# A second plain column block, the sums of activations after the attention, float32 gate tiles, and a scheduler that knows a shared SBUF interface

## The chip, the cores and the metric

The kernel runs on one core of a Trainium2 chip. The metric is the time on the device in microseconds (us), lower is better. TensorE is called PE here, VectorE DVE, ScalarE ACT, GpSimd POOL and SyncE SP, as in the profile.

## The reference

Causal attention, then two MLPs on the 896 tokens (2 batches of 448), all results in float32:

```python
# q, k, v: (2, 12, 448, 64)
scores = scale * np.matmul(q, k.transpose(0, 1, 3, 2))
scores = np.where(mask, -1000000000.0, scores)      # mask: upper triangle
attn = np.exp(scores - max); attn = attn / (sum + 1e-09)
x = np.matmul(attn, v)                              # to (896, 768)
g = x @ w_gate                                      # (768, 1536)
x = (g * (1.0 / (1.0 + np.exp(-g))) * (x @ w_val)) @ w_out    # (1536, 768)
h = x @ w_in                                        # (768, 2048)
out = (h * np.clip(h + 3.0, 0.0, 6.0) / 6.0) @ w_out2         # (2048, 768)
```

The weights come in float64 and are read as pairs of 32-bit words.

## The kernel before

**Number format.** A float32 operand of a matmul is split into a high part (fp32r) and a low part, the difference: ACT casts the high part, DVE or POOL subtracts it. A product of two split operands is three matmuls. A weight tile is loaded raw by SP (768 KB, two tiles `raw` that take turns), ACT scales its high words into `w`, DVE shifts `w` and joins the low words to it, and then it is split into `whi` and `wlo`.

**Attention.** 12 pairs of heads (6 of each batch), in steps woven by hand: scores `sc`, exponentials `e`, transposes `tp` and `et`, products `pv`, normalised rows `xn`, their transposes `tr` into 448 columns, split into the tiles `x` (`xt_parts`). For the MLP's Strassen form `xt_parts` also makes sums and differences of the `x` tiles: POOL adds the two parts of a tile into `xa` or `xb` (L627), DVE forms the differences (L631, L634 to L636), and the tiles `t1` are split there (`split_x`). The tile framework orders the instructions of this part by its own priorities.

**First layer (w_gate, w_val).** The 12 column blocks of 128 are planned in `mlps` by `Plan`: each operation is entered with the engines that may do it, its cost there, and what it reads and writes; PE's order is fixed as entered, due times are counted back from PE's, and a list scheduler places every other operation on the engine where it can start first, earliest due first. From 9 us of the plan's own time on, the engines' queues keep that order. Column block 0 (`PLAIN = 1`) is plain: gate and value, each of two batches, 18 matmuls of 448 columns each, 72 in all. Its two weight tiles are loaded and prepared in the attention (`UNIT_AT`). Blocks 1 to 11 are in Strassen-Winograd form: the 2 by 2 split is batches by halves of the 768 inputs and gate by value; 7 products of 9 matmuls, 63 in all, in the order a11 (x tiles), s3 with `t3`, s2 with `t2`, s1 with `t1`, a12, a22 with `t4`, s4. Their weight operands come from `operands`: 4 sums and 7 splits of 384 columns on DVE or POOL for each block. The results are combined on DVE (`tmp`, `mm`) and gated (`silu` on ACT, then a product). For the first four blocks (`EARLY = 4`) the gate's result is split at once from PSUM; for the others it is kept as a float32 tile `g` and split at the end of the layer (`g_parts`) into `gh` and `gl`.

**The rest.** The layer of w_out is planned too (6 column blocks, in two parts of 384 and 512 tokens); the second MLP is written in order, with the next weight tiles made ahead.

Instructions of the planned part have the line of the helper `InOrder`, L53, whatever they do; they are told apart by their tiles. The scheduler's main rule is this one, for each engine e:

```python
t = max(free_at[e], min(at[i] for i in mine))
i = min((i for i in mine if at[i] <= t), key=lambda i: (due[i], i))
```

Of the kernel before, what the change touches and what calls it, by code (L numbers as in the profile page):

```python
# [69 lines left out]
class Plan:  # L70
# [4 lines left out]
    def op(self, where, call, reads=(), writes=()):  # L75
# [19 lines left out]
        self.ops.append((where, call, before, ready))  # L95

    def run(self, emit):
# [3 lines left out]
        for i, (_, _, before, _) in enumerate(ops):  # L101
            for j in before:
                after[j].append(i)
# [3 lines left out]
        for i, (where, _, _, _) in enumerate(ops):  # L107
# [11 lines left out]
        free_at = dict(START)  # L119
# [4 lines left out]
        while waiting:  # L124
            best = None
            for e in free_at:
# [7 lines left out]
                t = max(free_at[e], min(at[i] for i in mine))  # L134
                i = min((i for i in mine if at[i] <= t), key=lambda i: (due[i], i))
# [5 lines left out]
            free_at[e] = t + cost  # L141
            if e in ("pe", "sp"):
                (pe_order if e == "pe" else sp_order).pop(0)
            placed.append((t, len(placed), i, e))
            for j in after[i]:
                left[j] -= 1
                at[j] = max(at[j], t + cost + LAG[e])
# [9 lines left out]
def tile_attention_glu_mlp(  # L157
# [123 lines left out]
    for f in range(PLAIN):  # L281
        units.append((cols(w_gate, f), KD, 128))
        units.append((cols(w_val, f), KD, 128))
# [41 lines left out]
    xs = {}  # L325
# [23 lines left out]

    def split_x(k, h, by):  # L350

        (xa, _), (xb, _) = sums[h], more_sums[h]
        src = {1: xb[:, 1], 2: xa[:, 0], 3: xa[:, 1], 4: xb[:, 0]}[k]
        xs[k, h] = pair_tile(f"t{k}{h}")
        t = xs[k, h][0]
        act.copy(t[:, 0], src)
        by.tensor_tensor(out=t[:, 1], in0=src, in1=t[:, 0].bitcast(F32), op=ALU.subtract)

    def attention():
        with ExitStack() as st:  # L360
# [241 lines left out]
            def xt_parts(p):  # L602
# [7 lines left out]
                def one(c):  # L610
# [12 lines left out]
                    h = hp % HD  # L623
                    (xa, _), (xb, _) = sums[h], more_sums[h]
# [50 lines left out]
    def mlps():  # L675
# [41 lines left out]
        def floats(src, name):  # L717
# [27 lines left out]
            plan.op({"vec": 0.75}, shift, writes=[w])  # L745
            plan.op({"vec": 1.15}, join, reads=[raw], writes=[w])
            return w

        def parts_of(src, hi, lo, size, both=True):
# [6 lines left out]
            where = {"vec": 0.08 + size * 0.0012}  # L756
            if both:
                where["pool"] = 0.1 + size * 0.0027
# [5 lines left out]
                reads=[(s, s_part), (h, h_part)], writes=[(l, l_part)],  # L764
            )

        def combine(where, out, in0, in1, op):
# [4 lines left out]
                reads=[a[:2], b[:2]], writes=[o[:2]],  # L772
# [8 lines left out]
        x1s = [[here(x1[b][k], 6.5 if (b, k) == (1, KD - 1) else 0.0) for k in range(KD)] for b in range(B)]  # L781
        t1 = [here(xs[1, h], 2.0) for h in range(HD)]
        xa = [here(sums[h], 7.8 if h == HD - 1 else 0.0) for h in range(HD)]
        xb = [here(more_sums[h], 7.8 if h == HD - 1 else 0.0) for h in range(HD)]
# [6 lines left out]
        def gate(f, b, bank_, in0, in1):  # L791
# [9 lines left out]
            parts_of(at(bank_, None, tok), at(hi, b, mid), at(lo, b, mid), S, both=False)  # L801
# [37 lines left out]
        def operands(f):  # L839
# [5 lines left out]
            either = {"vec": 0.65, "pool": 1.2}  # L845
# [7 lines left out]
            combine(either, s1, a21, a22, ALU.add)  # L853
            piece("a11", a11)
            combine(either, a21, a11, a21, ALU.subtract)
            piece("s3", a21)
            combine(either, s2, s1, a11, ALU.subtract)
# [3 lines left out]
            combine(either, a12, a12, s2, ALU.subtract)  # L861
# [4 lines left out]
        g_tiles(0)  # L866
        ws = [[Spot(real=t) for t in made[u]] for u in range(2)]
        used[0] += 2
        for b in range(B):
            got = []  # L870
            for wh, wl in ws:
                t, n = bank_spot()
                got.append((t, n))
                plan.op(
                    {"pe": 3 * KD * PE448},
                    lambda e, t=t, wh=wh, wl=wl, b=b: mm3(
                        tok(t()),
# [190 lines left out]
```

## Time and profile before

| | |
|---|---|
| time, median of 3 runs | 609.87 us (609.69 to 610.8) |
| the profiled execution's own time | 610.62 us |
| its span | 608.5 us |
| mean granted clock of PE | 0.994 |
| busy share: PE, DVE, ACT, POOL | 98%, 63%, 48%, 41% |
| chain that ended last, largest shares | PE 80%, DVE 12%, POOL 3%, issue 2% |
| read from HBM | 61.73 MB |

The profile is of one execution. The span runs from its first to its last instruction; the execution's own time includes what lies around that. A window is given in us from the span's start. "Idle before" is the time that the engine sat without work before an instruction, and the name behind the arrow is what ended it. An x9 in a timeline merges nine instructions of one kind.

### The profile page before, as it was taken

How to read it: one execution, taken by the hardware profiler on the slowest of the kernel's cores; microseconds unless marked ns; L12 is line 12 of the kernel's file. 1: busy time of each engine (PE TensorE's matmuls, PEld its weight loads, DVE VectorE, ACT ScalarE, POOL GpSimd, SP SyncE). 2: the span in 40 equal slices, each digit the busy share in tenths (PEclk: the TensorE clock that was granted, in tenths of full speed). 3: DMA queues.
4: the chain of work that ended last, by engine and by line, in shares of the span. 5: the costliest groups of instructions: out<-in, count | busy, mean ns of one | idle time of the engine just before them, and what ended most of it. 6: DMA issues, size and time to landing. Idle time of an engine off the chain costs nothing.

```text
span 608.5 us, 9429 instructions
## 1 busy us (share of the span) xinstructions
PE 595.2 (98%) x3519; PEld 551.1 (91%) x3519; DVE 382.1 (63%) x741; ACT 293.6 (48%) x530; POOL 246.8 (41%) x194
## 2 busy tenths in 40 slices
PE   8999999997999999999999999999999999999997
PEld 5999998886999998989888889999888899999997
DVE  6889899889999999989754443544555531123001
ACT  5677786665655645547432224555555532223000
POOL 4566766267658877748100002222222222223200
PEclk9999999997999999999999999999999999999999
DMA  9555546044334435341543343333333343342002
GB/s 180 131 127 141 135 104 173 13 155 140 108 106 155 157 111 181 124 156 53 160 156 111 120 121 106 108 106 103 104 103 104 104 110 111 118 156 66 1 0 92
DMA packets 83918, 70.15 MB, mean 115 GB/s; under 512 B 35232, under 2 KB 79776, under 8 KB 83872
## 3 DMA queue, kind: packets, MB, share of 16 engines
q1 hardware_dynamic: 83872, 69.55, 39.5%
q8 instruction: 28, 0.46, 0.3%
q14 instruction: 18, 0.15, 0.1%
HBM read 61.73 MB, written 2.75 MB: 106 GB/s over the span
## 4 chain that ended last, share of the span: by engine, by line
PE 80%; DVE 12%; POOL 3%; issue 2%; ACT 1%; DMA 0%; SPq 0%; DVEq 0%; ACTq 0%; POOLq 0%
PE mm L53 65%; PE pv L580 5%; PE sc L509 4%; PE tp L552 3%; DVE w L53 2%; DVE v L53 2%; POOL s L53 1%; DVE s L53 1%; PE tr L434 1%; DVE tmp L53 1%; POOL a L53 1%; DVE e L522 1%; DVE qq L447 1%; PE tr L614 1%; DVE mm L53 1%
## 5 line engine op out<-in xcount | busy, mean ns | idle before, releaser
L53 POOL TENSOR_TENSOR wlo<-w,whi 128x768 fp32r<-128x768 f32 (+1 forms) x33 | 59.4, 1801 | 243.9 <-PE mm L53 219.6
L53 DVE TENSOR_SCALAR w<-w 128x768 uint32<-128x768 uint32 (+1 forms) x58 | 39.7, 685 | 79.3 <-ACT w L53 78.7
L53 ACT CAST whi<-w 128x768 fp32r<-128x768 f32 (+1 forms) x47 | 38.5, 818 | 78.8 <-PE mm L53 72.7
L53 PE MATMUL mm<-whi,g2l 128*128 128x384 f32 x224 | 74.8, 334 | 0.0
L53 PE MATMUL mm<-whi,g2h 128*128 128x384 f32 x224 | 74.8, 334 | 0.0
L53 PE MATMUL mm<-wlo,g2h 128*128 128x384 f32 x224 | 74.8, 334 | 0.0
L580 PE MATMUL pv<-v,et 112*112 112x65 f32 x480 | 73.5, 243 | 0.8 <-DVE et L558 0.8
L53 PE MATMUL mm<-x2h,wlo 128*128 128x384 f32 (+1 forms) x192 | 69.9, 364 | 0.0
L53 PE MATMUL mm<-x2l,whi 128*128 128x384 f32 (+1 forms) x192 | 69.8, 364 | 0.0
L53 PE MATMUL mm<-x2h,whi 128*128 128x384 f32 (+1 forms) x192 | 69.6, 362 | 0.0
L53 PE MATMUL mm<-t,s 128*128 128x448 f32 x297 | 65.6, 378 | 3.5 <-ACT s L53 2.1
L580 PEld LDWEIGHTS pv<-v,et 112*112 112x112 f32 x480 | 65.5, 177 | 2.2 <-DVE et L558 1.0
L53 PEld LDWEIGHTS mm<-t,s 128*128 128x128 f32 x297 | 57.5, 194 | 9.9 <-ACT s L53 2.5
L53 ACT ACTIVATE w<-raw 128x768 f32<-128x768 f32 (+1 forms) x58 | 51.5, 890 | 29.5 <-POOL wlo L53 19.2
L552 PE MATMUL tp<-ident,e 112*112 112x112 f32 x240 | 61.1, 260 | 2.3 <-ACT e L532 2.2
L53 DVE SCALAR_TENSOR_TENSOR w<-raw,w 128x768 uint32<-128x768 uint32 (+1 forms) x58 | 59.7, 1029 | 0.9
L532 ACT ACTIVATE e<-e,m 112x336 f32<-112x336 f32 (+1 forms) x96 | 48.7, 531 | 20.8 <-DVE m L522 20.6
L53 PE MATMUL mm<-gh,wlo 128*128 128x384 f32 (+1 forms) x144 | 52.5, 364 | 0.0
L53 PE MATMUL mm<-gl,whi 128*128 128x384 f32 (+1 forms) x144 | 52.4, 364 | 0.0
L53 PE MATMUL mm<-gh,whi 128*128 128x384 f32 (+1 forms) x144 | 52.2, 362 | 0.0
L53 PE MATMUL mm<-x,a 128*128 128x448 f32 x198 | 44.2, 367 | 0.0
L522 DVE CUSTOM_DVE_ANT_0 e<-sc,mask 112x336 f32<-112x336 f32 (+1 forms) x96 | 40.7, 445 | 4.5 <-PE sc L509 2.6
(126 smaller groups left out, 1322.6 us busy)
## 6 DMA issues: line engine op xcount, KB each, us to landing
raw<-in_moe_w_out_dram SPq DMA_DIRECT2D x28, 768.0 KB, 4.3
raw<-in_moe_w_in_dram SPq DMA_DIRECT2D x16, 768.0 KB, 4.5
raw<-in_moe_w_gate_dram SPq DMA_DIRECT2D x12, 768.0 KB, 4.2
raw<-in_moe_w_val_dram SPq DMA_DIRECT2D x12, 768.0 KB, 5.6
kn<-in_k_dram SPq DMA_DIRECT2D x24, 112.0 KB, 2.6
qn<-in_q_dram SPq DMA_DIRECT2D x24, 112.0 KB, 2.6
v<-in_v_dram SPq DMA_DIRECT2D x12, 224.0 KB, 3.2
out_dram<-ob SPq DMA_DIRECT2D x14, 192.0 KB, 1.8
```

Of the source, the lines that this page charges most:

```text
L53: ins = call(*args, **kw)
L434: nc.tensor.transpose(tr[:, c * C : (c + 1) * C], n[:, c].rearrange("p j d -> p (j d)"), ident[:C, :C])
L447: nc.vector.tensor_copy(hi[r, j, :], f[r, :])
L509: nc.tensor.matmul(sp[:C, o : o + w], t["qq"][:, j, c * C : (c + 1) * C], t[("kk", "k2")[i]][:, j, 0:w], start=(i == 0), stop=(i == 1),)
L522: nc.vector.tensor_tensor_reduce(out=es, in0=sp[:C, o : o + w], in1=mask[:, S - w :], op0=ALU.add, op1=ALU.min, scale=-SCALE, scalar=3.0e3 ...
L532: nc.scalar.activation(out=es, in_=es, func=AF.Exp, scale=-1.0, bias=m[:, x : x + 1])
L552: nc.tensor.transpose(tp[:C, at - lo : at - lo + C], e[:, at : at + C], ident[:C, :C])
L580: nc.tensor.matmul(box["o"][:, qc, :], et[:, at : at + C], vt[:, j, c, :], start=(c == 0), stop=(c == qc))
L614: nc.tensor.transpose(tr[:, c * C : (c + 1) * C], xn[:, c].rearrange("p j d -> p (j d)"), ident[:C, :C])
```

## The change

Five things change.

1. `PLAIN = 2`: column block 1 is plain too. Its weight tiles are loaded and split in the plan (`unit`), not in the attention.
2. The sums of activations leave the attention. `xt_parts` now copies each transposed tile on ACT into `xa` or `xb` (12 copies) and makes one difference on DVE for half of the pairs of the second batch. The other nine differences and the splits of `t1` are operations of the plan, on DVE or POOL.
3. `EARLY = 0`: every gate tile is kept in float32 and split by `g_parts`.
4. The planner has a flag `port` on the operations that read and write SBUF alone: of these only one runs at a time, on DVE or on POOL. Its costs of DVE and POOL operations, the start times and the due times between PE operations are other numbers.
5. `unit` and the plain block become functions used for both cases.

```diff
-PLAIN = 1
+PLAIN = 2
-START = {"act": 5.6, "vec": 7.9, "pool": 7.0, "pe": 0.0, "sp": 0.0}
+START = {"act": 6.5, "vec": 7.2, "pool": 7.3, "pe": 0.0, "sp": 0.0}
-EARLY = 4
+EARLY = 0
...
+                t = min(t + LAG["pe"], due[j]) if "pe" in ops[i][0] and "pe" in ops[j][0] else t
...
-                t = max(free_at[e], min(at[i] for i in mine))
-                i = min((i for i in mine if at[i] <= t), key=lambda i: (due[i], i))
+                starts = {i: max(free_at[e], at[i], port_free if ops[i][4] else 0.0) for i in mine}
+                t = min(starts.values())
+                i = min((i for i in mine if starts[i] <= t), key=lambda i: (due[i], i))
...
+            if ops[i][4]:
+                port_free = t + cost
...
-                    whole = xa[:, b] if hp < HD else xb[:, 0] if b == 0 else None
-                    if whole is not None:
-                        nc.gpsimd.tensor_tensor(
-                            out=whole, in0=x[:, 0].bitcast(F32), in1=x[:, 1].bitcast(F32), op=ALU.add
-                        )
+                    xa, xb = sums[hp % HD][0], more_sums[hp % HD][0]
+                    nc.scalar.copy((xa if hp < HD else xb)[:, b], src)
                     if b == 1 and hp < HD:
-                        nc.vector.tensor_tensor(out=xb[:, 1], in0=src, in1=xa[:, 0], op=ALU.subtract)
-                        split_x(1, h, pool)
-                    if b == 1 and hp >= HD:
-                        nc.vector.tensor_tensor(out=xa[:, 0], in0=src, in1=xb[:, 1], op=ALU.subtract)
-                        nc.vector.tensor_tensor(out=xa[:, 1], in0=src, in1=xa[:, 1], op=ALU.subtract)
-                        nc.vector.tensor_tensor(out=xb[:, 0], in0=xb[:, 0], in1=xa[:, 0], op=ALU.subtract)
+                        nc.vector.tensor_tensor(out=xa[:, 0], in0=src, in1=xa[:, 0], op=ALU.subtract)
...
+        plain(0, [[Spot(real=t) for t in made[u]] for u in range(2)])
         used[0] += 2
+        for f in range(1, PLAIN):
+            plain(f, [unit(cols(w, f), both=True) for w in (w_gate, w_val)])
+        tk = {}
+        for h in range(HD):
+            f1, f2, f3, f4 = at(xa[h], 0, nth(0)), at(xb[h], 1, nth(1)), at(xa[h], 1, nth(1)), at(xb[h], 0, nth(0))
+            by = {"vec": 0.58, "pool": 1.25}
+            combine(by, f3, f2, f3, ALU.subtract, port=True)
+            combine(by, f2, f2, f1, ALU.subtract, port=True)
+            combine(by, f4, f4, f2, ALU.subtract, port=True)
+            for k, src in ((1, f1), (3, f3), (2, f2), (4, f4)):
                 t = take([128, 2, S], F32R, f"t{k}{h}")
                 parts_of(src, at(t, 0, nth(0)), at(t, 1, nth(1)), S)
-                tk[k].append(t)
+                tk.setdefault(k, []).append(t)
...
-        for f in range(1, K1):
+        for f in range(PLAIN, K1):
```

How the built program's queues move, at three places.

*First: DVE at the end of the attention* (`x` is the split of a transposed tile, `et` the copy of a transposed exponential that the next `pv` reads, `w` the first weight tile in halves). Before:

```order
L53 TENSOR_TENSOR x_1877<-tr_1837,x_1877 128x448
L634 TENSOR_TENSOR xa_68<-tr_1837,xb_71 128x448
L635 TENSOR_TENSOR xa_68<-tr_1837,xa_68 128x448
L636 TENSOR_TENSOR xb_71<-xb_71,xa_68 128x448
L53 TENSOR_SCALAR w<-w 128x384
L558 COPY et<-tp_1906 112x336
L53 SCALAR_TENSOR_TENSOR w<-raw,w 128x384
L590 TENSOR_SCALAR r<-pv_1904 112x4
```

With the change:

```order
L53 TENSOR_TENSOR x_1868<-tr_1828,x_1868 128x448
L552 COPY et<-tp_1895 112x336
L53 TENSOR_SCALAR w<-w 128x384
L584 TENSOR_SCALAR r<-pv_1893 112x4
L53 SCALAR_TENSOR_TENSOR w<-raw,w 128x384
L586 RECIPROCAL ri<-r 112x4
L53 TENSOR_TENSOR xa_68<-xb_71,xa_68 128x448
L587 TENSOR_TENSOR xn<-pv_1893,ri 112x4x64
```

The three differences of `xa` and `xb` are gone from between the split of `x` and the copy `et`; one difference stands five places behind `et`.

*Second: ACT at the start of the plain block* (`whi` is the cast of a weight tile, in two halves of 384 and then one of 768; `tmp<-mm` is the silu of the first plain product). Before:

```order
L53 CAST x_1953<-tr_1939 128x448
L53 ACTIVATE w<-raw 128x768
L53 CAST whi<-w 128x384
L53 ACTIVATE w<-raw 128x384
L53 CAST whi<-w 128x384
L53 CAST whi<-w 128x768
L53 CAST x_1974<-tr_1969 128x448
L53 ACTIVATE w<-raw 128x768
L53 CAST t_2036<-xa_68 128x448
```

With the change:

```order
L53 CAST whi<-w 128x384
L53 ACTIVATE w<-raw 128x384
L53 CAST t_2047<-xa_68 128x448
L53 CAST x_1942<-tr_1928 128x448
L53 CAST whi<-w 128x384
L618 COPY xb_72<-tr_1928 128x448
L53 ACTIVATE w<-raw 128x768
L53 CAST x_1961<-tr_1956 128x448
L53 CAST t_2050<-xa_69 128x448
L53 ACT_TABLE_LOAD
L53 ACTIVATE tmp_2044<-mm_1977 128x448
L53 CAST whi<-w 128x768
```

The load of ACT's function table and the first silu now stand ahead of the cast of the second weight tile; before, they stood 17 places behind it.

*Third: PE in the attention, a stretch that returns in six pairs of heads* (`sc` scores, `tr` transposes of k and q, `tp` of exponentials). Before:

```order
L434 MATMUL tr_565<-ident,kn 128x112
L509 MATMUL sc_576<-kk_103,qq_102 112x224
L509 MATMUL sc_576<-k_104,qq_102 112x224
L552 MATMUL tp_580<-ident,e 112x112
L580 MATMUL pv_559<-v_2_115,et 112x65
L552 MATMUL tp_580<-ident,e 112x112
L509 MATMUL sc_576<-kk_103,qq_102 112x224
L434 MATMUL tr_600<-ident,qn 128x112
L580 MATMUL pv_559<-v_2_115,et 112x65
L552 MATMUL tp_603<-ident,e 112x112
L580 MATMUL pv_559<-v_2_115,et 112x65
L509 MATMUL sc_576<-k_104,qq_102 112x224
```

With the change:

```order
L428 MATMUL tr_565<-ident,kn 128x112
L546 MATMUL tp_580<-ident,e 112x112
L574 MATMUL pv_559<-v_2_115,et 112x65
L546 MATMUL tp_580<-ident,e 112x112
L428 MATMUL tr_600<-ident,qn 128x112
L574 MATMUL pv_559<-v_2_115,et 112x65
L503 MATMUL sc_576<-kk_103,qq_102 112x224
L503 MATMUL sc_576<-k_104,qq_102 112x224
L503 MATMUL sc_576<-kk_103,qq_102 112x224
L546 MATMUL tp_603<-ident,e 112x112
L574 MATMUL pv_559<-v_2_115,et 112x65
L503 MATMUL sc_576<-k_104,qq_102 112x224
```

Three score matmuls now stand behind five others; the fourth has its old place. On POOL the queue shrinks from 146 to 93 rows, on DVE it grows from 721 to 751, on ACT from 530 to 537; SP's order is the same.

## Rows read from the trace of the kernel before

**Rows 1.** The page, part 1: busy time, share of the span and instructions of each engine.

```profile
PE 595.2 (98%) x3519; PEld 551.1 (91%) x3519; DVE 382.1 (63%) x741; ACT 293.6 (48%) x530; POOL 246.8 (41%) x194
```

**Rows 2.** The waits of PE: who waited for whom, us in total, times, longest.

```profile
PE tp L552 <- ACT e L532: 2.2, 4, 0.9
```

**Rows 3.** Stretches: length, busy us of PE, PEld, DVE, ACT, POOL, clock, DMA, GB/s.

```profile
15.00:50.00 35.00, 34.90 (x349) 34.02 (x347) 29.91 (x112) 25.72 (x59) 22.70 (x19) 1.00 0.57 135
118.40:134.60 16.20, 15.66 (x80) 13.84 (x79) 14.40 (x19) 8.70 (x16) 9.94 (x8) 1.00 0.36 107
134.60:148.30 13.70, 10.24 (x37) 8.42 (x36) 12.87 (x17) 8.12 (x14) 8.36 (x7) 0.75 0.38 125
148.30:284.80 136.50, 135.47 (x658) 123.09 (x658) 128.83 (x171) 78.51 (x146) 95.40 (x77) 1.00 0.43 137
```

**Rows 4.** The same table, a stretch behind the wait.

```profile
141.00:144.00 3.00, 3.00 (x8) 2.70 (x9) 3.00 (x4) 0.99 (x2) 1.93 (x2) 0.50 0.00 0
```

**Rows 5.** Timeline of PE: start, length, operation, count, idle time before it.

```profile
118.42 0.65 PE L53 MATMUL mm<-x,whi 128*128 128x448 f32 x2
...
134.58 1.98 PE L53 MATMUL mm<-x,a 128*128 128x448 f32 x9
138.64 0.91 PE L53 MATMUL mm<-t,s 128*128 128x448 f32 x2 [2.08 <-ACT s L53]
140.93 7.56 PE L53 MATMUL mm<-t,s 128*128 128x448 f32 x25 [1.38 <-DVE s L53]
148.33 2.02 PE L53 MATMUL mm<-x,a 128*128 128x448 f32 x9
...
161.35 2.02 PE L53 MATMUL mm<-x,a 128*128 128x448 f32 x9
...
242.32 2.09 PE L53 MATMUL mm<-t,a 128*128 128x448 f32 x9 [1.03 <-DVE tmp L53]
...
283.00 1.99 PE L53 MATMUL mm<-x,s 128*128 128x448 f32 x9
284.83 0.33 PE L53 MATMUL mm<-gh,whi 128*128 128x384 f32 x1
```

**Rows 6.** Timelines of PE and DVE near the end of the attention.

```profile
94.79 0.31 PE L552 MATMUL tp<-ident,e 112*112 112x112 f32 x1 [0.67 <-ACT e L532]
...
114.02 0.61 DVE L634 TENSOR_TENSOR xa<-tr,xb 128x448 f32<-128x448 f32 x1
114.55 0.61 DVE L635 TENSOR_TENSOR xa<-tr,xa 128x448 f32<-128x448 f32 x1
...
115.88 0.50 DVE L558 COPY et<-tp 112x336 f32<-112x336 f32 x1
...
116.43 2.18 PE L580 MATMUL pv<-v,et 112*112 112x65 f32 x20 [0.78 <-DVE et L558]
```

**Rows 7.** Timelines of POOL and DVE in the plain block.

```profile
126.36 5.51 POOL L53 TENSOR_TENSOR t<-xa,t 128x448 fp32r<-128x448 f32 x4 [0.66 <-ACT t L53]
...
130.78 1.91 DVE L53 SCALAR_TENSOR_TENSOR w<-raw,w 128x768 uint32<-128x768 uint32 x1
132.61 0.94 DVE L53 SCALAR_TENSOR_TENSOR v<-raw,v 128x768 uint32<-128x768 uint32 x1
```

**Rows 8.** Timeline of ACT, one pair of heads in the attention.

```profile
78.30 0.53 ACT L440 COPY f<-tr 128x448 f32<-128x448 f32 x1 [0.53 <-PE tr L434]
...
83.58 0.58 ACT L532 ACTIVATE e<-e,m 112x336 f32<-112x336 f32 x1 [1.14 <-DVE m L522]
```

**Rows 9.** Timeline of ACT at the table load.

```profile
136.35 1.28 ACT L53 ACT_TABLE_LOAD   x1
137.65 0.54 ACT L53 ACTIVATE tmp<-mm 128x448 f32<-128x448 f32 x1
```

**Rows 10.** The page, part 5: the splits of weight tiles on POOL; busy us, mean ns.

```profile
L53 POOL TENSOR_TENSOR wlo<-w,whi 128x768 fp32r<-128x768 f32 (+1 forms) x33 | 59.4, 1801 | 243.9 <-PE mm L53 219.6
```

**Rows 11.** The loads of weight tiles, from the answer on the tile raw.

```profile
DMA to landing us min/median/max: 4.0/4.5/6.5
```

More of the change, by code (lines that the diff above doesn't have):

```diff
@@ L94, in op @@
         before.discard(i)
-        self.ops.append((where, call, before, ready))
+        self.ops.append((where, call, before, ready, port))
     def run(self, emit):
@@ L100, in run @@
         after = [[] for _ in range(n)]
-        for i, (_, _, before, _) in enumerate(ops):
+        for i, (_, _, before, _, _) in enumerate(ops):
             for j in before:
@@ L106, in run @@
         due = [None] * n
-        for i, (where, _, _, _) in enumerate(ops):
+        for i, (where, _, _, _, _) in enumerate(ops):
             if "pe" in where:
@@ L280, in tile_attention_glu_mlp @@
     units = []
-    for f in range(PLAIN):
+    for f in range(1):
         units.append((cols(w_gate, f), KD, 128))
@@ L348, in mm3 @@
             part()
[L350 to L357, printed above, removed]
     def attention():
@@ L743, in join, with parts_of @@
                 )
-            plan.op({"vec": 0.75}, shift, writes=[w])
-            plan.op({"vec": 1.15}, join, reads=[raw], writes=[w])
+            plan.op({"vec": 0.6}, shift, writes=[w], port=True)
+            plan.op({"vec": 1.02}, join, reads=[raw], writes=[w], port=True)
             return w
-        def parts_of(src, hi, lo, size, both=True):
+        def parts_of(src, hi, lo, size, both=True, port=True):
             (s, s_part, s_ap), (h, h_part, h_ap), (l, l_part, l_ap) = src, hi, lo
@@ L779, in nth @@
             return lambda t: t[:, i]
[L781 to L784, printed above, removed]
+        x1s = [[here(x1[b][k], 6.0 if (b, k) == (1, KD - 1) else 0.0) for k in range(KD)] for b in range(B)]
+        xa = [here(sums[h]) for h in range(HD)]
+        xb = [here(more_sums[h], 6.0 if h == HD - 1 else 0.0) for h in range(HD)]
         temps = [take([128, 2, S], F32, f"tmp{i}") for i in range(3)]
@@ L864, in operands @@
             return out
-        g_tiles(0)
-        ws = [[Spot(real=t) for t in made[u]] for u in range(2)]
-        used[0] += 2
[L869 to L877, printed above, removed]
-                        [(wh()[:, k], wl()[:, k], x1s[b][k]()[:, 0], x1s[b][k]()[:, 1]) for k in range(KD)],
-                    ),
-                    reads=[wh, wl] + x1s[b], writes=[t],
-                )
-            silu(at(sg, b, nth(b)), got[0][0])
-            gate(0, b, got[1][0], at(got[1][0], None, tok), at(sg, b, nth(b)))
-            idle.extend(n for _, n in got)
@@ L885, in mlps, with unit, plain @@
-        tk = {1: t1}
-        for k in (3, 2, 4):
-            tk[k] = []
-            for h in range(HD):
-                src = {2: at(xa[h], 0, nth(0)), 3: at(xa[h], 1, nth(1)), 4: at(xb[h], 0, nth(0))}[k]
+        def unit(src, both=False):
+            w = floats(src, "w")
+            hi, lo = (ring_spot("ws", [128, KD, 128], F32R, n) for n in ("whi", "wlo"))
+            parts_of(at(w), at(hi), at(lo), KD * 128, both=both)
+            return hi, lo
+        def plain(f, ws):
+            g_tiles(f)
+            for b in range(B):
+                got = []
+                for wh, wl in ws:
+                    t, n = bank_spot()
+                    got.append((t, n))
+                    plan.op(
+                        {"pe": 3 * KD * PE448},
+                        lambda e, t=t, wh=wh, wl=wl, b=b: mm3(
+                            tok(t()),
+                            [(wh()[:, k], wl()[:, k], x1s[b][k]()[:, 0], x1s[b][k]()[:, 1]) for k in range(KD)],
+                        ),
+                        reads=[wh, wl] + x1s[b], writes=[t],
+                    )
+                silu(at(sg, b, nth(b)), got[0][0])
+                gate(f, b, got[1][0], at(got[1][0], None, tok), at(sg, b, nth(b)))
+                idle.extend(n for _, n in got)
@@ L921, in mlps @@
             idle.extend((nx, ny, nz, nw))
-        def unit(src):
-            w = floats(src, "w")
-            hi, lo = (ring_spot("ws", [128, KD, 128], F32R, n) for n in ("whi", "wlo"))
-            parts_of(at(w), at(hi), at(lo), KD * 128, both=False)
-            return hi, lo
         give(*b11, *tk[3], *tk[2], *tk[1], *b21, *tk[4], *b22)
@@ L961, in mlps @@
                 src = at(pt, None, lambda t, size=size: t[:, :size])
-                parts_of(src, at(x2s[e][0], part.start, mid), at(x2s[e][1], part.start, mid), size, both=False)
+                parts_of(src, at(x2s[e][0], part.start, mid), at(x2s[e][1], part.start, mid), size, both=False, port=False)
             idle.extend(n for _, n in pts.pop(e))
```

31 lines of the change are left out of this document (14 added, 17 removed).

## The prediction

> **What bounds the kernel now.** The page is read first: TensorE (PE) is busy for 595.2 of 608.5 us [rows 1], so an edit pays only where PE waits, where its clock is down, or where it has fewer columns to stream. A busy PE is no proof that each matmul runs at its best, so the second view is the waits of PE (its longest line is [rows 2]) and the third the table of stretches with the granted clock [rows 3]. There one stretch stands out, 134.6 to 148.3: the clock is 0.75 and PE is busy for 10.24 of 13.70 us. The finer table [rows 4] shows a clock of 0.50 over 141 to 144, that is 1.2 instead of 2.4 GHz, with PE busy throughout. PE's timeline [rows 5] says what it is: the plain column block runs from 118.42 to 134.58, the first Strassen block issues its first product (9 matmuls), and then waits 2.08 us for a ScalarE (ACT) cast and 1.38 us for a VectorE (DVE) subtraction of its second product's operand s; 25 matmuls at the low clock follow, to 148.33.
>
> What a matmul of 448 columns costs: from 148.33 to 284.83 PE does 657 of them (10 blocks of 63 and the last 27 of block 1), 136.50 us less the one wait of 1.03 before 242.32 [rows 5], so 0.206 us each. Single blocks vary: 63 in 148.33 to 161.35 are 0.2067 each, 9 in 283.00 to 284.83 are 0.2033. No row shows why; I keep both for the range.
>
> The profiled execution took 610.62 us, 0.75 more than the median of 609.87. The sum below is made against 610.62, and the 0.75 is taken off at its end. "No change" here means within 0.2%, 1.2 us.
>
> **The change, part by part.**
>
> *1. The hole closes: -6.3.* From 134.58 to 148.33 PE spent 13.75 us on 36 matmuls worth 36 x 0.206 = 7.42 [rows 5]. With a second plain block in between, the first Strassen product is due 144 matmuls, 29.7 us, after the first plain one (call that moment T0), not 14.8. Is everything ready by then? The moved sums and splits now stand in DVE's queue behind T0. I walk that queue in the changed order, with steps as the rows have them when GpSimd (POOL) is not in the way: 0.53 for 448 columns (114.02 to 114.55) [rows 6] and 0.47 for 384 (by width), 0.5 for the shift of a weight tile, 0.9 for its join (132.61, lasting 0.94) and 0.9 for its split. Up to the last split of the second product's operands DVE has, from T0 on, 6 shifts and joins (one pair of half size), 2 splits of weight tiles, 13 operations of 448 columns and 6 of 384: some 20 us of work (7.7 + 1.8 + 6.9 + 2.8, and 0.5 of small ones), and 4 to 6 us of waiting for x and for loads, so T0+24 to T0+26, for a product due at T0+31.6. POOL can stretch this: while it ran four subtractions without a break from 126.36 on, DVE's join of 130.78 took 1.91, against 0.94 for the next one, with POOL idle [rows 7]. So a collision costs up to 1 us; but the changed order leaves POOL only 6 operations in this whole stretch, so at most 6 us more. That would use up the slack, not exceed it much. I take the hole as closed; ends of this term: -6.3 and -2.3 (see the first rival).
>
> *2. Nine more matmuls: +1.85.* A plain block is 72 matmuls, a Strassen block 63; 9 x 0.206. Nothing covers them, PE is the bound.
>
> *3. The wait of 1.03 in the middle of the Strassen stretch goes: -1.0.* It is PE waiting for DVE's tmp [rows 5], while DVE is busy 128.83 of 136.50 us there [rows 3], collisions included. The change takes from DVE in this stretch the 8 splits of gate halves, and from POOL about half of its operations, so that DVE runs nearer to its uncontended steps. Ends: -1.0 and 0.
>
> *4. The end of the attention: -1.2.* PE waits 2.2 us for ACT's e [rows 2], in the first microseconds and near the attention's end, 0.67 of it before 94.79; and 0.78 before 116.43 for DVE's copy et [rows 6]. That copy stands at 115.88 behind three subtractions L634 to L636 that begin at 114.02; the changed queue has it directly behind the split of x (first order piece), so these 1.6 us no longer stand in front of it and I count 0.7. Before 94.79 the removed POOL operations (one sum and one split of t) had delayed POOL's k and qq subtractions, with which DVE's casts collide; I count 0.5 for this and the like wait at 104. Nine additional ACT copies of about 0.48 us come in (12 new ones, 3 casts of t gone). They are costed at nothing: in each pair of heads ACT sits idle 0.53 us for PE's transposes and 1.14 us for DVE's m [rows 8], and the copy falls just ahead of the first. If that cover fails, see the second rival. Ends: -1.9 and +1.
>
> *5. The start of the plain block: -0.3.* In 118.4 to 134.6 PE has 72 matmuls, 14.8 us, in 16.2; transposes take some 0.5, so about 0.9 is waiting. In the changed ACT queue the table load, and the silu that needs the first product complete, stand ahead of the cast whi of the second weight tile (second order piece). Walk: whi of the first tile's second half T0+1.8, copy and weight T0+3.0, x cast 3.5, t cast 4.0, load 5.3, silu 5.8, whi 6.7, and on POOL wlo, 1.8 us [rows 10], 8.5; PE asks for that wlo at about T0+8.1. So about 0.4 is lost there, and about 0.2 at the second half of the first tile: 0.6 in place of 0.9. Ends: -0.9 and +1. What the load costs is a row: 1.28 us, and the silu begins at once behind it, 137.65 [rows 9]. The Trainium skill (ScalarE: Activation LUTs, What ACT_TABLE_LOAD costs) has another price: a switch of table sets costs the load and a drain of some 1.38 us more, 2.66 us together. By that page, as an estimate, the wlo would come 1.4 us later and this term would be +1.1. The row shows no such gap, so the sum goes by 1.28.
>
> *6. Edits at nothing.* Gate tiles in float32: 8 splits on ACT and DVE move from the first four blocks to the stretch around 284.8, where DVE and POOL have the other 16 already. The tiles of the first two blocks are split early; of the next four the last place comes free four products of 1.83 us [rows 5] before the first gate product, 7.3 us, and the order puts their 384-column parts on POOL, the others on DVE. PE asks for the last 512-column part some 6 us into the gate stage. Four extra splits at 0.5 to 1.2 us fit; if not, PE waits up to 1 us once. Loads: the order of SP is the same, each load waits for the join that frees its raw tile, and landing takes 4.0 to 6.5 us [rows 11].
>
> Sum: -6.3 + 1.85 - 1.0 - 1.2 - 0.3 = -6.95; 610.62 - 6.95 = 603.7 for an execution like the profiled one, and **602.9** for the median.
>
> **The rivals.**
>
> *The hole opens again, smaller, one block later.* The second plain block's weights are now made behind T0. The load of its w_val tile can be issued only when the join of the second tile is done, about T0+6, lands by T0+10 to T0+12.5 [rows 11], and ahead of the gate tile's wlo DVE has this tile's shift and join: wlo at T0+13.5 to T0+15.5, due at T0+15.5. For: a margin of 0 to 2 us, with collisions to come. Against: due times set the order, and the early rows of POOL are few. Price: a wait of about 1.5 us, and if the clock falls as it did after the waits of [rows 5], 25 matmuls at 7.40 instead of 5.15 us, 2.25 more: together 3.75, so 606.6. The same price would hold for operands that come late at T0+30.
>
> *Slower: ACT's copies reach PE in every pair.* The place is ACT's queue in the attention: the copy of x keeps the transposed bank longer, so three score matmuls now stand behind five others (third order piece). Then DVE's maxima, ACT's e and the next transposes come later. Price: 0.48 for the copy and 0.37 for five matmuls, 0.85 in each of 10 pairs, 8.5 us; with the 1.2 of part 4 not gained, 602.9 + 1.2 + 8.5 = 612.6. It decides from a delay of 0.6 us a pair on, where 10 pairs eat the gain. For: e lands close to its transposes. Against: PE is busy for 34.90 of the 35.00 us from 15 to 50 [rows 3], ACT has 1.7 us of idle time in a pair [rows 8], and the fourth score matmul of that group keeps its place in the queue.
>
> *The pitch.* If the whole Strassen stretch runs at 0.2033 instead of 0.206, 630 matmuls give 1.7 us more, 601.2; at 0.2067, 0.4 less. This belongs to the forecast's own range.
>
> That the change does nothing is excluded by the built order: PE has the second plain block, and the sums stand behind the attention.
>
> **How the numbers follow.** Forecast 0.71 (own range 600.4 to 605), the reopened hole 0.18 (605 to 608), slower by ACT's copies 0.07 (610 to 613), and 0.04 for mixtures that end within 0.2%. All of the first two are faster by over 0.2%, bar the 0.01 that I leave: faster 0.88, same 0.04, slower 0.08. The lower end of the range is the fast pitch with the better end of part 5; the upper end takes in most of the reopened hole: 600.4 to 606.8.
>
> **What would show it.** Right: no wait of PE over 0.5 us between the second plain block and the first Strassen block, clock 1.00 there, the first gate product some 29.7 + 129.8 + 1 = 160.5 us after the first plain matmul (166.41 before). Attention: PE's first plain matmul near 117.2. Wrong: a clock of 0.5 anywhere behind the start; plain matmuls waiting for wlo for more than 1 us; pairs of heads longer than before; ACT idle before the f copies gone and PE waiting for e. If the first Strassen block waits for s or t again, step 1 has failed.

## The result and the profile after

The changed kernel takes **601.59 us** (median of 4, 601.3 to 602.2) against 609.78 for the kernel before in the same comparison; the ratio is 0.9865, 95% interval 0.9848 to 0.9883. The forecast was 602.9. The profiled execution took 602.2, with a span of 600.4 and a mean granted clock of 0.999 (before 610.62, 608.5 and 0.994).

The page of after, part 1, to be read beside [rows 1]:

```profile
PE 593.0 (99%) x3528; PEld 551.0 (92%) x3528; DVE 372.3 (62%) x771; ACT 297.1 (49%) x536; POOL 176.7 (29%) x141
```

PE issues nine matmuls more and is busy for 2.2 us less; the 25 matmuls at half clock [rows 5] are gone. POOL lost 53 operations and 70 us.

Table of stretches of after (length, busy us of PE, PEld, DVE, ACT, POOL, clock, DMA, GB/s): the attention, the two plain blocks, the Strassen blocks.

```profile
15.00:50.00 35.00, 34.90 (x348) 34.01 (x347) 29.77 (x112) 26.63 (x61) 20.27 (x17) 1.00 0.59 135
117.00:148.30 31.30, 30.63 (x152) 27.25 (x151) 27.53 (x45) 21.30 (x36) 8.16 (x6) 1.00 0.47 152
148.30:276.80 128.50, 128.47 (x631) 118.03 (x630) 115.66 (x177) 69.51 (x132) 55.08 (x48) 1.00 0.36 117
```

Timeline of PE of after, to be read beside [rows 5]:

```profile
117.02 0.64 PE L53 MATMUL mm<-x,whi 128*128 128x448 f32 x2
...
125.88 0.47 PE L53 MATMUL mm<-x,wlo 128*128 128x448 f32 x1 [0.65 <-POOL wlo L53]
...
148.30 2.02 PE L53 MATMUL mm<-x,a 128*128 128x448 f32 x9
150.16 5.74 PE L53 MATMUL mm<-t,s 128*128 128x448 f32 x27
...
161.32 2.02 PE L53 MATMUL mm<-x,a 128*128 128x448 f32 x9
163.18 5.94 PE L53 MATMUL mm<-t,s 128*128 128x448 f32 x27
...
274.98 1.99 PE L53 MATMUL mm<-x,s 128*128 128x448 f32 x9
276.80 0.34 PE L53 MATMUL mm<-gh,whi 128*128 128x384 f32 x1
```

Where 138.64 and 140.93 carried waits before, the nine and the 27 products now follow each other without a bracket, at clock 1.00, and one wait over 0.2 us is left between T0 = 117.02, the start of the first plain matmul, and the gate products: 0.65 for a weight tile's low part. The 8.05 us of span add up from the two traces: the first score product 0.13 earlier (scatter: in two executions of one program, e2 and e9, it starts at 8.09 and 8.54); the pairs of heads up to 85 us 0.26 longer together (8.84 each in place of 8.80); the attention's tail from there to the first plain matmul 1.53 shorter (31.74 in place of 33.27); the first 72 plain matmuls 0.24 longer (16.40, 16.16); the second plain block 14.88 new; the Strassen stretch 21.75 shorter (128.50, 150.25); the rest the same within 0.02. The 21.75 in turn: one block less 12.98, the hole 6.3, the wait of 1.03, and 1.4 because the matmuls came at 0.2040 each and not at 0.206. By e9 a difference of that size can come from the execution alone; no run shows the change to have made it.

### The profile page after: what moved, and what is told of

The parts are those of the page before. It is cut to its first block, busy times and chain, and to the rows that moved or that the text cites. A ratio compares the mean times of both kernels' runs of the same rounds, so it can differ in the third digit from the quotient of the medians.

```text
span 600.4 us, 9398 instructions
## 1 busy us (share of the span) xinstructions
PE 593.0 (99%) x3528; PEld 551.0 (92%) x3528; DVE 372.3 (62%) x771; ACT 297.1 (49%) x536; POOL 176.7 (29%) x141
## 4 chain that ended last, share of the span: by engine, by line
PE 94%; DVE 4%; ACT 1%; DMA 0%; issue 0%; POOL 0%; SPq 0%; ACTq 0%; DVEq 0%
PE mm L53 78%; PE pv L574 5%; PE sc L503 4%; PE tp L546 3%; PE tr L428 1%; DVE e L516 1%; DVE qq L441 1%; PE tr L608 1%; DMA kn<-in_k_dram 0%; POOL wlo L53 0%; DVE xn L587 0%; PE zero L367 0%; DVE et L552 0%; PE tr L458 0%; ACT L53 0%
## 5 line engine op out<-in xcount | busy, mean ns | idle before, releaser
L53 DVE TENSOR_SCALAR w<-w 128x768 uint32<-128x768 uint32 (+1 forms) x59 | 35.6, 604 | 79.6 <-ACT w L53 76.6
L53 ACT CAST whi<-w 128x768 fp32r<-128x768 f32 (+1 forms) x49 | 40.1, 819 | 66.5 <-PE mm L53 57.4
L53 DVE SCALAR_TENSOR_TENSOR w<-raw,w 128x768 uint32<-128x768 uint32 (+1 forms) x59 | 57.3, 971 | 0.8
L53 PE MATMUL mm<-t,s 128*128 128x448 f32 x270 | 57.0, 366 | 0.0
L53 PEld LDWEIGHTS mm<-t,s 128*128 128x128 f32 x270 | 50.5, 188 | 4.9 <-DVE s L53 0.9
L53 PEld LDWEIGHTS mm<-whi,g2h 128*128 128x128 f32 x224 | 42.0, 188 | 0.0
```

What stands on the lines that cost most here:

```text
L53: ins = call(*args, **kw)
```

## The experiments

The theory at the start was the prediction's: the second plain block is 15 us of cover under which DVE, ACT and POOL make the first Strassen operands, the moved sums give the attention's end, and the gate tiles and the scheduler's rules are worth little alone. The rival: one of those "little" edits carries the gain. Ratios are to the kernel before, with 95% intervals.

**e1: one plain block in the changed kernel.**

```diff
-PLAIN = 2
+PLAIN = 1
```

> The changed kernel with one plain column block instead of two; the sums stay out of the attention and the scheduler keeps its new rules. Theory (the second plain block's 15 us of matmuls are the cover under which VectorE, ScalarE and GpSimd make the first Strassen operands): the hole ahead of the first Strassen block comes back, 6 us or more, since the sums now fall in it too; nine matmuls fewer take 1.85 off, so 605 to 610 us. Rival (the sums' new place and the scheduler's rules close the hole by themselves): no TensorE wait over 0.5 us there and 599.5 to 600.5 us.

Measured 606.84 (0.9956, 0.9936 to 0.9976). Within the theory's 605 to 610, but not as it drew it: no single hole of 6 us, but many waits of up to 1.3 us, spread over the first four Strassen blocks, at a mean granted clock of 1.00. One of the waits:

```profile
146.35 1.69 PE L53 MATMUL mm<-t,a 128*128 128x448 f32 x7 [1.31 <-DVE a L53]
```

The order spreads the shortage; the block is worth 5.2 us here. So it isn't the block alone either: 3.0 us are gained without it.

**e2: the sums back in the attention** (two plain blocks, new scheduler, late gate tiles kept).

```diff
-                    nc.scalar.copy((xa if hp < HD else xb)[:, b], src)
...
+                        nc.vector.tensor_tensor(out=xa[:, 0], in0=src, in1=xb[:, 1], op=ALU.subtract)
+                        nc.vector.tensor_tensor(out=xa[:, 1], in0=src, in1=xa[:, 1], op=ALU.subtract)
+                        nc.vector.tensor_tensor(out=xb[:, 0], in0=xb[:, 0], in1=xa[:, 0], op=ALU.subtract)
...
-        tk = {}
+        tk = {1: t1}
```

> The changed kernel with the sums and the first split put back into the attention as they were, two plain blocks and the new scheduler kept. Theory (the sums' place is worth 1.2 us at the attention's end and nothing behind it): first plain matmul back at 118.2 to 118.5 us, the last two head pairs at 9.4 us or more instead of 9.16, the stretch from the first plain matmul to the first gate product unchanged at 159.8, and 602.5 to 603.2 us. Rival (the end of the attention got shorter by the order alone, not by the sums' work): first plain matmul stays near 117.0 and the time within 0.3 of 601.6. A second rival (the ACT copies cost 0.04 us in each pair): the steady pairs go back from 8.84 to 8.80.

Measured 601.42 (0.9867, 0.9841 to 0.9894): no loss, and so below the theory's 602.5 to 603.2; the profiled execution, 603.97, was the slowest of the four. The attention's end does get longer again (first plain matmul 117.94, expected 118.2 to 118.5; last pairs 9.72 and 9.44), and the steady pairs go back to 8.80, as the second rival had it. But the first 72 plain matmuls take 15.55 instead of 16.40, without a wait for wlo, and the first Strassen product comes at 148.37, against 148.30. Counted from the first score product, that is 140.28 against 139.77 us: the place of the sums is worth about half a microsecond, which the times don't show. Most of what the attention's end gains, the start of the plain block loses; ACT gets to it later there (its table load comes at T0+1.7 in e2 and at T0+4.3 in the change).

**e3: four gate tiles split at once again.**

```diff
-EARLY = 0
+EARLY = 4
```

> The changed kernel with the first four gate tiles split at once again, as before the change. Theory (the gate tiles' float32 form is worth nothing by itself): 601.3 to 602.1 us and no TensorE wait over 0.5 us between the plain blocks and the gate products beyond that at 125.9. Rival (the 1.03 us wait in the middle of the Strassen stretch went because VectorE lost these early splits): one wait of 0.5 to 1 us comes back and 602.3 to 603 us.

Measured 605.07 (0.9917, 0.9897 to 0.9938): 3.5 us lost, more than either side expected. Timeline of PE of e3, and its table for three us behind the wait (granted clock 0.51):

```profile
164.01 0.67 PE L53 MATMUL mm<-t,s 128*128 128x448 f32 x2 [1.52 <-ACT s L53]
165.16 6.90 PE L53 MATMUL mm<-t,s 128*128 128x448 f32 x25 [0.48 <-DVE s L53]
```

```profile
166.00:169.00 3.00, 3.00 (x10) 2.65 (x9) 2.96 (x6) 1.24 (x4) 0.00 (x0) 0.51 0.03 5
```

The hole is there again, one block later, with the low clock behind it: 25 matmuls in 6.90 us instead of 5.15. A gate tile that is split at once puts one ACT cast and one DVE subtraction for each half among the operands of the next block; in float32 the same splits wait for free places, on POOL too.

**e4: the port rule out of the scheduler.**

```diff
-starts = {i: max(free_at[e], at[i], port_free if ops[i][4] else 0.0) for i in mine}
+starts = {i: max(free_at[e], at[i]) for i in mine}
```

> The changed kernel with the scheduler blind to the shared interface again (the costs, starts and due times stay the new ones). Theory (with two plain blocks there is slack, so the collisions of VectorE and GpSimd are hidden): 601.3 to 602.3 us, though GpSimd's busy time between the plain blocks and the first gate product goes up from 55 us and VectorE's steps beside it stretch. Rival (the plan that keeps VectorE and GpSimd apart is what closes the hole): a TensorE wait of 1 us or more ahead of the first Strassen blocks and 603 us or more.

Measured 615.17 (1.0083, 1.0064 to 1.0103): 13.6 us slower than the change, slower than the kernel before, and far past the rival's mark. Timelines of PE and DVE of e4:

```profile
166.10 3.73 PE L53 MATMUL mm<-t,a 128*128 128x448 f32 x9 [4.61 <-DVE tmp L53]
...
160.52 2.78 DVE L53 TENSOR_TENSOR gl<-g,gh 128x384 fp32r<-128x384 f32 x2
```

Two splits of a gate tile, 0.55 each with POOL idle, take 2.78 beside POOL, ahead of the tmp for which PE waits 4.61. With the new low costs and no rule, the scheduler believes it has room that isn't there; that is my reading of these rows.

This turned the theory round: the scheduler is what the other edits stand on. The next three runs take it from the other end, from the kernel before.

**e5: the kernel before with a second plain block, nothing else.**

```diff
-PLAIN = 1
+PLAIN = 2
...
+        for f in range(1, PLAIN):
+            plain(f, [unit(cols(w, f), both=True) for w in (w_gate, w_val)])
```

> The kernel before with a second plain column block and nothing else: old scheduler rules and costs, sums in the attention, four gate tiles split at once. Theory after the first four runs (the block is the cover, but it closes the hole only together with the scheduler's port rule and the late gate tiles): TensorE waits of 1 to 3 us in all remain between the plain blocks and the third Strassen block, 604.5 to 608 us. Rival (my forecast's term 1: the block alone closes the hole): no wait over 0.5 us there and 602 to 603.5 us. Second rival (without the port rule the collisions eat all that the block gives): 609 us or more.

Measured 611.17 (1.0023, 1.0011 to 1.0035): the second rival, 1.3 us slower than before. Timelines of PE, POOL and DVE of e5:

```profile
136.01 0.47 PE L53 MATMUL mm<-x,wlo 128*128 128x448 f32 x1 [1.66 <-DVE wlo L53]
...
126.39 7.34 POOL L53 TENSOR_TENSOR t<-xa,t 128x448 fp32r<-128x448 f32 x5
...
127.95 2.94 DVE L53 TENSOR_SCALAR w<-w 128x768 uint32<-128x768 uint32 x2
130.81 3.75 DVE L53 SCALAR_TENSOR_TENSOR w<-raw,w 128x768 uint32<-128x768 uint32 x2
...
162.96 3.59 PE L53 MATMUL mm<-t,a 128*128 128x448 f32 x9 [3.38 <-DVE tmp L53]
...
156.33 1.39 POOL L53 TENSOR_TENSOR s<-s,w 128x384 f32<-128x384 f32 x1
157.67 1.33 POOL L53 TENSOR_TENSOR s<-s,s 128x384 fp32r<-128x384 f32 x1
158.97 1.31 POOL L53 TENSOR_TENSOR a<-w,a 128x384 fp32r<-128x384 f32 x1
160.36 1.19 POOL L53 TENSOR_TENSOR w<-w,s 128x384 f32<-128x384 f32 x1
...
156.76 1.37 DVE L53 TENSOR_SCALAR w<-w 128x768 uint32<-128x768 uint32 x1
158.05 1.37 DVE L53 TENSOR_TENSOR s<-v,s 128x384 fp32r<-128x384 f32 x1
159.34 1.36 DVE L53 TENSOR_TENSOR s<-s,s 128x384 fp32r<-128x384 f32 x1
160.62 0.61 DVE L53 TENSOR_TENSOR tmp<-mm,tmp 128x448 f32<-128x448 f32 x1
```

Read the two engines together. Under POOL's five t subtractions DVE's shifts take 1.47 and its joins 1.87 each (0.55 and 0.94 with POOL idle), and the second block's first wlo is 1.66 late: the first rival of the prediction, at its place and with the wait of 1.5 that it was priced at. From 156.33 on POOL and DVE go at one pace, one operation of each in 1.3 us. The tmp at 160.62, whose one input comes from PSUM (`mm`), takes its 0.61 while POOL works (160.36); but it stands behind three stretched ones. Behind the 3.38 the granted clock is 0.50 over 163.50 to 165.50. The Trainium skill (SBUF — State Buffer, Who interferes with whom) has GpSimd contend with DVE instructions that have two SBUF inputs or run in a two-port mode, and whichever comes second blocks for the whole of the other's instruction; the rows above agree, 1.37 for what takes 0.55 alone.

**e6: e5 with the late gate tiles as well** (EARLY = 0 in e5's kernel; it differs from e2 by the scheduler alone).

> The kernel before with the second plain block and the gate tiles in float32 to the layer's end, old scheduler, sums in the attention. It differs from the run with the sums put back only by the scheduler. Theory (the scheduler's port rule is needed even with the block and the late tiles): 1 us or more of waits, 603.5 to 606 us. Rival (the old, higher costs already held the collisions, so the port rule adds nothing): 601.3 to 602.5 us.

Measured 611.08 (1.0016, 1.0002 to 1.0031), above what both expected: four waits of PE for DVE's tmp, 5.3 us in all, and 1.5 for wlo. Late tiles give nothing under the old scheduler. e6 less e2 is the scheduler's worth beside the block and the late tiles: 9.7 us.

**e7: the kernel before with the new scheduler alone.** All of the change's edits in `Plan` and in the costs; PLAIN = 1, EARLY = 4, sums in the attention.

> The kernel before with the new scheduler alone (port rule, costs, starts and due times): one plain block, sums in the attention, four gate tiles split at once. Theory (without cover no order closes the hole, since the operands of the first Strassen block take longer than the 15 us of one plain block): first Strassen blocks still wait 4 to 7 us, 607 to 610.5 us. Rival (the old order was the cause of the hole): 604 us or less.

Measured 606.36 (0.9948, 0.9931 to 0.9965): 3.5 us faster, between the theory's range and the rival's. Timeline of PE of e7:

```profile
151.66 0.68 PE L53 MATMUL mm<-t,s 128*128 128x448 f32 x2 [2.22 <-ACT s L53]
152.97 6.89 PE L53 MATMUL mm<-t,s 128*128 128x448 f32 x25 [0.63 <-DVE s L53]
```

The first Strassen block now runs through after a single plain block (12.77 for its 63 matmuls); the hole is smaller and stands before the second one. So the old order was part of the cause. The rest is not the missing cover alone. With the new scheduler, a second block beside early gate tiles leaves the hole at 164.01 (e3, 605.1), and late tiles beside one block leave many waits (e1, 606.8); only the block and the late tiles together come to 601.4 to 602.0.

**e8: a version of mine.** The wait left in the changed kernel (125.88) is for POOL's wlo, which takes 1.83 and can begin only when ACT has done table load, silu and whi; DVE is idle at that time.

```diff
+        by = vec if len(made) == 1 else None
         made.append((hi, lo))
...
-            split_w(hi[:, p], lo[:, p], w[:, p])
+            split_w(hi[:, p], lo[:, p], w[:, p], by)
```

> The changed kernel with one edit of mine: the low part of the second prefetched weight unit is subtracted on VectorE, which stood idle from 122.4 to 125.2 us, and not on GpSimd, whose 1.83 us ended 0.65 us after TensorE asked. Theory (that wait is a join of ACT table load, silu, whi copy and GpSimd's subtraction, and goes with the last of them made shorter): the TensorE wait at 125.9 is gone, first Strassen matmul 0.6 to 1.0 us earlier, 600.6 to 601.1 us. Rival (the wait was cover for VectorE's operands, or the matmul pitch that it flips costs the same again): 601.4 to 602 us.

Measured 600.87 (0.9860, 0.9840 to 0.9880), the lowest median of all; its interval overlaps the change's, so the times don't show that it beats the change. Timelines of ACT, DVE and PE of e8:

```profile
122.95 0.84 ACT L53 CAST whi<-w 128x768 fp32r<-128x768 f32 x1
...
123.82 0.96 DVE L53 TENSOR_TENSOR wlo<-w,whi 128x768 fp32r<-128x768 f32 x1 [0.90 <-ACT whi L53]
...
146.73 1.98 PE L53 MATMUL mm<-x,a 128*128 128x448 f32 x9
```

wlo is there at 124.78 instead of 125.82, PE has no wait over 0.25 us from T0 to the gate products, and the 72 matmuls of the first plain block take 15.36 instead of 16.40. The first Strassen product comes 1.57 earlier, more than the 0.6 to 1.0 expected: 0.24 of that is an earlier T0, and about 0.4 is the matmuls' shorter spacing, 0.2027 for 0.2067, behind the place of the wait. The wait is gone, as the theory had it.

**e9: e2 again, for its matmul pitch.** No edit.

> The kernel with the sums put back in the attention once more, unchanged, for a second profiled execution: the first one ran all ten Strassen blocks at 13.02 us a block (0.2067 us a matmul) and took 603.97 us, its other executions 601.2 to 601.7. Theory (the matmul pitch has two levels, 0.2067 and 0.2028, and which one an execution keeps is decided at a small slip in TensorE's stream, not by the program): the same first plain matmul (117.8 to 118.3 us) and no wait behind it, and blocks either at 13.02 again (603.4 to 604.2 us) or at 12.77 for all or part of the stretch, each block of 12.77 taking 0.25 off. Rival (the program's order sets the pitch): 13.02 in all ten blocks again.

Measured 601.99 (0.9869, 0.9845 to 0.9892). Timelines of PE, the same 27 products, first of e2, then of e9:

```profile
150.23 5.74 PE L53 MATMUL mm<-t,s 128*128 128x448 f32 x27
```

```profile
150.57 5.63 PE L53 MATMUL mm<-t,s 128*128 128x448 f32 x27
```

Same program, same place, no wait in either, clock 1.00 in both: 13.02 us a block in one execution, 12.77 in the other. Over both plain blocks and the Strassen stretch that is 160.63 against 158.10. The rival, that the order sets the pitch, is out. One thing missed: the first plain matmul came at 118.74, outside the 117.8 to 118.3 expected, so with one and the same program T0 scatters by 0.8 us.

**e10: the copies of x made twice** (a second, equal `nc.scalar.copy` behind each).

> The changed kernel with each of the twelve float32 copies of x in the attention made twice on ScalarE (the same value to the same place), 0.53 us more in each pair. Theory (ScalarE keeps 1.4 us of idle time in a pair, so a copy costs what the order of the other work moves by, 0.04 us a pair): pairs at 8.84 to 8.95 and 601.6 to 602.9 us. Rival (my forecast's slower case, the et and exp steps behind the copies are late from 0.6 us a pair on): pairs at 9.2 us or more and 605 us or more.

Measured 611.05 (1.0018, 0.9998 to 1.0037), a time in the rival's range. The six steady pairs take 8.98 to 9.02, 0.15 more, near the theory; the last two take 12.67 each, 3.5 more. Timelines of PE and ACT of e10, and its table (granted clock 0.53) behind the first wait:

```profile
91.27 0.32 PE L574 MATMUL pv<-v,et 112*112 112x65 f32 x2
93.67 0.29 PE L608 MATMUL tr<-ident,xn 112*128 112x112 f32 x1 [2.08 <-DVE m L516]
...
93.24 1.32 ACT L526 ACTIVATE e<-e,m 112x112 f32<-112x112 f32 x3 [1.71 <-DVE m L516]
```

```profile
94.00:97.00 3.00, 3.00 (x21) 3.00 (x20) 0.51 (x1) 1.00 (x3) 0.35 (x1) 0.53 0.72 248
```

ACT is not full there: it is idle for 1.71 before that row, for DVE. What changed is the order that the scheduling layer made of the attention: the transposes of xn stand directly behind the products from which DVE must first make xn, with no scores between them, and PE waits 2.08 and 2.07 in the two pairs. The rest of the 3.5 lies behind the waits, where the clock is down. So a slower case exists in this kernel, at 3.5 us in a pair, but it is not the rival as I drew it: PE waits for DVE, behind a changed order, and not for an e that ACT makes late.

**e11: the old costs of DVE and POOL steps, port rule kept.**

```diff
-            plan.op({"vec": 0.6}, shift, writes=[w], port=True)
+            plan.op({"vec": 0.75}, shift, writes=[w], port=True)
...
-            either = {"vec": 0.52, "pool": 1.1}
+            either = {"vec": 0.65, "pool": 1.2}
```

> The changed kernel with the old, higher costs of VectorE's and GpSimd's steps in the scheduler, the port rule and the due times kept. Theory (the port rule is what keeps the two engines from stretching each other, the costs only shift its choices): waits of 1 us in all at most ahead of the gate products, 601 to 603 us. Rival (the truer costs are what closes the hole): waits of 2 us or more, 604 us or more.

Measured 604.96 (0.9925, 0.9897 to 0.9953): 3.4 lost, the rival. Timeline of PE of e11:

```profile
177.61 0.68 PE L53 MATMUL mm<-t,s 128*128 128x448 f32 x2 [1.53 <-ACT s L53]
178.70 6.88 PE L53 MATMUL mm<-t,s 128*128 128x448 f32 x25 [0.41 <-POOL s L53]
```

The hole is back, ahead of the third Strassen block's second product, with 25 matmuls in 6.88 us behind it (granted clock 0.51 over 179 to 182). Rule and costs belong together; that the old costs already held a share of the collisions, which the rule then counts again, is a reading of mine that no run here tests.

**e12: the old due times and lags.** The two lines on "pe" in `run` taken back.

> The changed kernel with the old rule of due times and of lags between TensorE's own steps, the port rule and the new costs kept. Theory (the due times only set the urgency along TensorE's own chain, and the port rule does the work): 601 to 603 us. Rival (the due times do the work): waits of 2 us or more ahead of the gate products and 604 us or more.

Measured 601.67 (0.9865, 0.9848 to 0.9882): no difference, as the theory had it. The other numbers that came with the new scheduler, the engines' start times and the times at which the first operands count as ready, were not run by themselves.

The parts side by side (medians; each run's before was 609.8 to 609.9):

| scheduler | plain blocks | gate tiles | sums | us |
|---|---|---|---|---|
| old | 1 | early | attention | 609.8 |
| old | 2 | early | attention | 611.2 |
| old | 2 | late | attention | 611.1 |
| new | 1 | early | attention | 606.4 |
| new | 1 | late | after it | 606.8 |
| new | 2 | early | after it | 605.1 |
| new | 2 | late | attention | 601.4, 602.0 |
| new | 2 | late | after it | 601.6 |

The old scheduler with one block and late tiles was not run.

## Why the prediction was right

The sign, the size and the marks of being right at its end came out: no wait over 0.5 us between the second plain and the first Strassen block, clock 1.00 there, the first gate product 159.8 us behind T0 (forecast 160.5), the first plain matmul at 117.02 (117.2). That the last is so close is luck in part, since T0 scatters by 0.8 us (e9). Of the marks of being wrong, one came out in small, pairs of heads longer by 0.04 us, and half of another: ACT's idle time before the f copies is gone (0.53 in [rows 8]), though PE waits for e less and not more (1.1 us in all, 2.2 in [rows 2]). Timeline of ACT of after:

```profile
78.39 0.53 ACT L434 COPY f<-tr 128x448 f32<-128x448 f32 x1
```

The prediction's reason for the largest term was only half right.

*1, the hole, -6.3: right in size, its cause too narrow.* The walk through DVE's queue held. Timeline of DVE of after:

```profile
126.28 1.79 DVE L53 SCALAR_TENSOR_TENSOR w<-raw,w 128x768 uint32<-128x768 uint32 x1
...
130.84 0.94 DVE L53 TENSOR_TENSOR wlo<-w,whi 128x768 fp32r<-128x768 f32 x1
131.71 0.61 DVE L53 TENSOR_TENSOR g<-mm,tmp 128x448 f32<-128x448 f32 x1
132.24 0.94 DVE L53 TENSOR_TENSOR wlo<-w,whi 128x768 fp32r<-128x768 f32 x1
133.10 1.57 DVE L53 TENSOR_TENSOR t<-xa,t 128x448 fp32r<-128x448 f32 x1
...
141.30 0.54 DVE L53 TENSOR_TENSOR s<-v,s 128x384 fp32r<-128x384 f32 x1
...
144.91 0.60 DVE L53 TENSOR_TENSOR t<-xa,t 128x448 fp32r<-128x448 f32 x1
```

The s of the second product is split at T0+24.8 (walked: T0+24 to T0+26), for a product issued at T0+33.1; the last t from xa, which the rows don't assign to the second or the fourth product, is done at T0+28.5. The gate tile's wlo is done at T0+14.8, inside the T0+13.5 to T0+15.5 of the first rival, and is first loaded into PE 1.9 later. But the walk took the changed order as given and put down the closing to the block. It was the new order, with POOL at 6 operations and the gate tiles deferred, that kept most of the walk's steps at their uncontended length. (Four of DVE's steps between 125.23 and 134.68 were stretched even so, by 3.2 us together, inside the 6 that the prediction allowed.) Under the old scheduler the same block opens two holes and costs 1.3 us (e5, e6).

*2, nine more matmuls, +1.85: right.* The second plain block took 14.88, 72 at 0.2067; a Strassen block at that pitch takes 13.02.

*3, the mid-stretch wait, -1.0: right in size, not in its reason.* None over 0.5 us is left there, and DVE is busy 115.66 of 128.50 us. But the moved gate splits aren't what did it: with them moved and the old scheduler PE waits four times for tmp (e6), and with them left early and the new scheduler it has no such wait (e7).

*4, the attention's end, -1.2: measured -1.40,* of which -1.53 is the tail, +0.26 the steady pairs and -0.13 an earlier start, which is scatter. "Costed at nothing" was wrong by that 0.26, and the cover I named for the copies, ACT's idle 1.7 us a pair, is no safe one in the last two pairs (e10).

*5, the start of the plain block, -0.3: measured +0.24.* Timelines of ACT and POOL of after:

```profile
121.35 1.28 ACT L53 ACT_TABLE_LOAD   x1
122.65 0.54 ACT L53 ACTIVATE tmp<-mm 128x448 f32<-128x448 f32 x1
123.09 0.83 ACT L53 CAST whi<-w 128x768 fp32r<-128x768 f32 x1
...
123.99 1.83 POOL L53 TENSOR_TENSOR wlo<-w,whi 128x768 fp32r<-128x768 f32 x1 [4.14 <-ACT whi L53]
```

whi ends at T0+6.9 (walked 6.7) and wlo at T0+8.8 (8.5), so the wait is 0.65 and not 0.4. The load takes 1.28 and the silu begins at once behind it; the further drain of 1.38 that the Trainium skill gives (ScalarE: Activation LUTs, What ACT_TABLE_LOAD costs) shows neither here nor in [rows 9], so the measurement decides. With the sums in the attention this wait doesn't exist (e2, e9): terms 4 and 5 are one trade, worth about half a microsecond.

*6, "edits at nothing": the step that failed.* The float32 gate tiles are worth 3.5 us in the changed kernel (e3). I asked only whether the moved splits fit at the layer's end, where they do, and not what they take from the operands' queue where they stood.

*The pitch, kept for the range,* came out at 0.2040 over the 630 matmuls, 1.3 us under the sum's 0.206; that is about the distance from 602.9 to 601.6. Since one program showed both spacings (e9), I call this part luck.

## What to carry to other kernels

When several edits come together, walk the queue once under the old order too: a step whose arithmetic holds only in the new order owes its gain to that order. The scheduler here needed both the contention of two engines as a rule and their uncontended costs: with the costs but not the rule the kernel lost 13.6 us (e4), with the rule but not the costs 3.4 us (e11), and more cover was worth nothing without them (e5, e6). Work with a late due time (the gate tiles' splits) should stay movable, on either engine.

## What the runs showed of the hardware

The 448-column matmuls came at one of two spacings, 0.2067 or 0.2027 us (13.02 or 12.77 for 63), with the same program, granted clock 1.00 and no wait (e2 and e9); over the 774 matmuls from the first plain one to the gate products that made 2.5 us. In the traces an execution keeps its spacing for many blocks and mostly changes it at a small slip in PE's stream: the changed kernel ran at 0.2027 up to the wait of 0.65 at 125.88, at 0.2067 behind it, and from a slip of 0.2 at 163.4 at 0.2027 again, almost to the end. e2 changed to 0.2067 at 126.3 without a slip that the trace shows. What decides between the two stays open.

The clock fell behind some waits and not behind others: to 0.50 or 0.51 after 1.52 and 0.48 in short order (e3) and after 3.38 (e5), and to 0.53 after 2.08 (e10), while e6 with a wait of 2.56 at 162.38 kept 1.00. Table of e5, then timeline and table of e6:

```profile
163.50:165.50 2.00, 2.00 (x7) 1.78 (x6) 1.97 (x4) 0.00 (x0) 0.00 (x0) 0.50 0.94 291
```

```profile
162.38 2.09 PE L53 MATMUL mm<-t,a 128*128 128x448 f32 x9 [2.56 <-DVE tmp L53]
```

```profile
162.00:165.00 3.00, 2.62 (x13) 2.45 (x14) 3.00 (x5) 0.51 (x1) 1.65 (x2) 1.00 0.01 3
```
